# A gated scan followed by a multiplicative FFN on one core: a new hand-written order of 2,449 steps and a new split of side work between engines

## Chip, core and metric

The kernel runs on one core of one Trainium2 chip. The metric is the device time of one execution in microseconds. Three executions of the kernel before took 511.65, 510.97 and 511.06 us; their median is 511.06 us.

## What is computed

Four sequences of 5,824 tokens with 256 channels go through a gated linear recurrence (a scan in time, channel by channel), and its output through a feed-forward part with two parallel up-projections to 1,024 columns that are multiplied, then two further matrices. Cut to what matters:

```python
# scan, per channel: c = 8, a_base = sigmoid(a_param)
a_t  = exp(c * sigmoid(r_gate) * log(a_base))
xg   = sqrt(max(1 - a_t*a_t, 1e-6)) * sigmoid(i_gate) * x
h    = a_t[:, t] * h + xg[:, t];   y[:, t] = h
# feed-forward, on y as (23296, 256)
out  = ((y @ w1) * (y @ w2)) @ w3 @ w_out
```

All inputs and the output are f32; the matrix work is done in bf16.

## The kernel before

The 23,296 tokens are cut into 47 chunks: two of 256 tokens (0 and 1), 44 of 512, one of 256. A chunk's gate inputs `r`, `i` and `x` are loaded with tokens on the partitions (512 KB each). ScalarE (ACT) takes tanh of `r` and `i`; GpSimd (POOL) adds one to the tanh of `i` (`plus`) and multiplies it with `x` (`times`, L192), with VectorE (DVE) as an alternative; `th_r` and `u` are turned to channels on the partitions, by TensorE (PE, L200) for some of the first eight chunks and by a transposing DMA for all others. ACT makes the decay `a_t` by exp (L223); its square comes from POOL, DVE or ACT (`square`, L231 and L233, chosen by `DV_SQUARE` and `AC_SQUARE`); ACT takes the root (L238). Exp and tanh share a function table on ACT, the root needs another, so a switch shows as an ACT_TABLE_LOAD. DVE multiplies the root with `u` (`gated`, L248 and L251), then runs the scan, two instructions for the two halves of the channels (L270), each from the last column of the chunk before. `cast` makes `y` in bf16 (L282 on POOL or DVE, L280 on ACT).

The feed-forward part multiplies `w3 @ w_out` once, in the first 45 us (eight fold steps), into `wp_sb`. After that a chunk needs on PE eight matmul pairs for `y @ w1` (`pa`), eight for `y @ w2` (`pb`, both L299) and four strips of eight for the last product (`po`, L357). Each `pa` is copied to SBUF in bf16 (`copy`, L320 on DVE where `DV_COPY` names it, else L322 on ACT), DVE multiplies the copy with `pb` (`product`, L337), and `po` is copied out (`evac`) and stored.

Nothing schedules at run time. The string `ORDER` lists all steps; a loop at the end of the kernel runs through it and emits each step's instructions, so that the string gives the order on each engine and on SyncE's (SP) DMA queue. Each engine works strictly through its own list and waits at an instruction until its inputs are there and its buffer is free. `a5.1.0` is the `pa` matmuls of chunk 5, pair 1, half 0; `c` is its copy, `b5.1` the `pb` matmuls of that pair, `m` the product, `D` a strip of the last product, `e` its evacuation, `o` its store; `r i x` are loads, `R I p t V U` the gate steps up to the turned tiles, `d s q g h y` decay, square, root, gating, scan and cast; `Lw.. Cw..` load and cast a piece of the weights, `Ft Fc Fm Fe` fold; `W` is a pair of warming matmuls whose result nobody reads. Buffers are rings: `pa`, the turned tiles, the folds and `po` share four PSUM buffers (`po`), `pb` and the warming matmuls two (`pb`), staged weights share rings `a` and `nrm` with the decays and the roots.

Of the kernel before, what the change touches and what calls it, by code (L numbers as in the profile page):

```python
# [23 lines left out]
def kernel(  # L24
# [449 lines left out]
    def last(c):  # L474
# [26 lines left out]
        Lw3.4 x3 Lw3.3 Lw3.6 Lw3.7 r7 m0.2 h2.0 h2.1 R3 a1.2.1 a1.2.0 a0.3.0 c1.3.0 c0.3.0 Fm2 b0.3 b1.2 V3 R4 V4
        c1.2.0 d3.1 d4.0 d3.0 d4.1 m0.3 b1.3 y2 Fe2 m1.2 m1.3 a2.0.0 a2.0.1 b2.0 a2.1.0 c2.0.1 c2.0.0 c2.1.0 m2.0
        Cw3.0 s3.1 Cw3.5 Cw3.1 b2.1 a2.2.1 Ft0 a2.1.1 Fc0 Ft1 c2.1.1 Fc1 s4.0 I3 s4.1 c2.2.1 a2.2.0 Ft5 Fm0 p3 Cw3.4
        c2.2.0 Fc5 m2.1 s3.0 q3 Cw3.3 Fe0 b2.3 Fm1 q4 Fe1 Ft4 t3.0 t3.1 U3 Fc4 g3 h3.0 h3.1 Cw3.6 Cw3.7 b2.2 Fm5 Fm4
        a2.3.1 Ft7 R7 Fe5 Fe4 Fc7 r5 i4 r6 x4 i5 i6 i7 c2.3.1 a2.3.0 Ft3 R5 I4 c2.3.0 Fc3 Ft6 Fm7 y3 a3.2.1 Fc6 Fm3
# [159 lines left out]
```

## Time and profile before

| what | us |
|---|---|
| median of the three timed executions | 511.06 |
| span of the profiled execution, first to last instruction | 509.1 |
| difference, which lies around the span | 1.96 |
| PE busy (matmuls) | 501.7 |
| ACT busy | 461.5 |
| DVE busy | 431.8 |
| POOL busy | 318.0 |

How to read it: the span is one execution, recorded by the profiler; what lies around it is taken to be the same for both kernels. A busy time is the union of an engine's instructions; matmul ends are modelled. In a timeline row the first number is the start in us from the span's start, the second the length of a run of like instructions, `x` their count, and a bracket gives the idle time ahead and who ended it.

### The profile page before, as it was taken

To read this page: it belongs to the slowest core of one execution; us is meant where nothing else is said; L and a number is where in the kernel's file an instruction comes from. 1 tells how busy PE (TensorE), PEld (TensorE's weight loads), DVE (VectorE), ACT (ScalarE), POOL (GpSimd) and SP (SyncE) were. 2 spreads that over 40 slices of the span, in tenths; PEclk is the share of its full clock that TensorE was granted. 3 is DMA by queue.
4 is the path that set the end of the run, shared out by engine and by line. 5 is a ranking of instruction groups with operands and counts; after the bars stand their busy time and mean duration, and the time that the engine had idled before them with its cause. 6 is when DMAs were issued, how large, how long until landed. Compare 5 with 4: busy or idle time off the path is not lost.

```text
span 509.1 us, 8891 instructions
## 1 busy us (share of the span) xinstructions
PE 501.7 (99%) x3225; PEld 308.3 (61%) x3225; DVE 431.8 (85%) x417; ACT 461.5 (91%) x708; POOL 318.0 (62%) x269
## 2 busy tenths in 40 slices
...
GB/s 317 410 411 345 335 316 282 305 286 259 310 220 298 279 285 247 211 302 196 247 305 327 254 286 148 252 243 227 210 246 164 235 298 161 85 166 62 65 51 104
DMA packets 178048, 124.06 MB, mean 244 GB/s; under 512 B 87378, under 2 KB 174036, under 8 KB 178004
## 3 DMA queue, kind: packets, MB, share of 16 engines
...
q10 hardware_dynamic: 4, 0.00, 0.0%
...
## 4 chain that ended last, share of the span: by engine, by line
PE 92%; ACT 3%; DMA 2%; POOL 1%; DVE 1%; issue 1%; SPq 1%; ACTq 0%; DVEq 0%
PE po L357 30%; PE pb L299 29%; PE pa L299 29%; DMA wf<-in_moe_w_dram 2%; PE pw L436 1%; ACT sa L322 1%; PE ptr L200 1%; PE ptw L425 1%; POOL u_t L192 0%; DVE h_t L270 0%; SPq L151 0%; ACT ot L322 0%; SPq L407 0%; ACT L168 0%; ACT L238 0%
## 5 line engine op out<-in xcount | busy, mean ns | idle before, releaser
L337 DVE TENSOR_TENSOR g_t<-sa,pb 128x1024 bf16<-128x1024 bf16 (+1 forms) x188 | 218.7, 1180 | 58.9 <-PE pb L299 27.6
L299 PEld LDWEIGHTS <-w_sb 128*128 128x128 bf16 x1504 | 146.4, 98 | 144.1 <-issue 1.4
L322 ACT CAST sa<-pa 128x512 bf16<-128x512 f32 (+1 forms) x332 | 179.8, 591 | 27.1 <-PE pa L299 18.9
L299 PE MATMUL pa<-y_t,w_sb 128*128 128x512 bf16 (+1 forms) x752 | 190.2, 372 | 0.2 <-ACT sa L322 0.2
L299 PE MATMUL pb<-y_t,w_sb 128*128 128x512 bf16 (+1 forms) x752 | 184.9, 372 | 0.2 <-ACT w_sb L414 0.2
L357 PE MATMUL po<-wp_sb,g_t 128*128 128x256 bf16 (+1 forms) x1464 | 177.6, 272 | 0.0
L357 PEld LDWEIGHTS <-g_t 128*128 128x128 bf16 x1464 | 142.5, 98 | 39.5 <-issue 0.3
L282 POOL CAST y_t<-h_t 128x1024 bf16<-128x1024 f32 (+2 forms) x47 | 53.8, 1145 | 140.2 <-DVE h_t L270 136.1
L192 POOL TENSOR_TENSOR u_t<-i_t,x_t 128x512 bf16<-128x512 f32 (+1 forms) x90 | 123.3, 1387 | 3.8 <-DMA ut<-u_t 1.8
L270 DVE TENSOR_TENSOR_SCAN h_t<-a_t,h_t,nrm 128x512 f32<-128x512 f32 (+1 forms) x92 | 121.1, 1343 | 1.6
L233 POOL TENSOR_TENSOR nrm<-a_t 128x512 f32<-128x512 f32 x70 | 78.4, 1137 | 7.0 <-ACT a_t L223 4.0
L223 ACT ACTIVATE a_t<-rt,la 128x512 f32<-128x512 bf16 (+1 forms) x82 | 66.1, 823 | 0.0
L322 ACT COPY ot<-po 128x512 f32<-128x512 f32 x84 | 49.1, 589 | 13.2 <-PE po L357 12.9
L173 POOL TENSOR_SCALAR i_t<-i_t 128x1024 f32<-128x1024 f32 (+1 forms) x45 | 55.4, 1233 | 8.3 <-ACT i_t L168 8.3
L251 DVE SCALAR_TENSOR_TENSOR nrm<-nrm,ut 128x1024 f32<-128x1024 f32 (+1 forms) x39 | 53.2, 1365 | 5.2 <-ACT nrm L238 5.2
L168 ACT ACTIVATE i_t<-i_t 128x1024 f32<-128x1024 f32 (+1 forms) x46 | 48.5, 1063 | 0.3 <-DMA i_t<-in_i_gate_dram 0.2
L238 ACT ACTIVATE nrm<-nrm 128x1024 f32<-128x1024 f32 (+1 forms) x47 | 48.4, 1040 | 0.2
L162 ACT ACTIVATE th_r<-r_t 128x1024 bf16<-128x1024 f32 (+1 forms) x41 | 43.5, 1064 | 0.0
L320 DVE CAST sa<-pa 128x512 bf16<-128x512 f32 x36 | 23.5, 684 | 1.4 <-PE pa L299 0.8
L238 ACT ACT_TABLE_LOAD x17 | 21.8, 1283 | 0.4
L287 PE MATMUL warm<-ident 128*128 128x512 bf16 x32 | 10.7, 473 | 1.6 <-DVE ident L441 1.6
L231 ACT ACTIVATE nrm<-a_t 128x512 f32<-128x512 f32 x18 | 11.4, 645 | 0.0
...
## 6 DMA issues: line engine op xcount, KB each, us to landing
...
wf<-in_moe_w_dram SPq DMA_DIRECT2D x12, 512.0 KB, 10.5
...
rt<-th_r SPq DMA_TRANSPOSE x41, 4.7
ut<-u_t SPq DMA_TRANSPOSE x39, 4.4
```

Source lines behind the costliest of these rows:

```text
L173: (nc.vector if c in DV_PLUS else nc.gpsimd).tensor_scalar(t, t, 1.0, 1.0, op0=ALU.add, op1=ALU.mult)
L192: (nc.vector if (c, half) in DV_HALF else nc.gpsimd).tensor_mul(out=u, in0=t, in1=xt)
L223: nc.scalar.activation(out=a, in_=pr, func=AF.Exp, scale=la4[:, cb:cb + 1], bias=la4[:, cb:cb + 1])
L233: (nc.vector if (c, cb) in DV_SQUARE else nc.gpsimd).tensor_mul(out=n, in0=a, in1=a)
L238: nc.scalar.activation(out=n, in_=n, func=AF.Sqrt, scale=-1.0, bias=1.0)
L251: nc.vector.scalar_tensor_tensor(out=n, in0=n, scalar=1e-3, in1=T["pu", c][:, :, cols], op0=ALU.max, op1=ALU.mult)
L270: nc.vector.tensor_tensor_scan(h[:, cb, :], a[:, cb, :], n[:, cb, :], init, ALU.mult, ALU.add)
L282: (nc.vector if key in DV_CAST else nc.gpsimd).tensor_copy(out=y, in_=h)
L299: nc.tensor.matmul(out=dst, lhsT=w_sb[:, cb, m * P:(m + 1) * P], rhs=T["y", gates_of(c)][:, cb, span(c, mp)], start=(cb == 0), stop=(cb == ...
L322: nc.scalar.copy(out=dst, in_=src_ps)
L337: nc.vector.tensor_mul(out=T["g", z][:, 2 * mp:2 * mp + 2, span(c, mp)], in0=T["sa", c, mp][:, :, :w], in1=T["pb", c, mp][:, :, :w])
L357: nc.tensor.matmul(out=po, lhsT=T["g", c][:, k, j * P:(j + 1) * P], rhs=wp_sb[:, k, cols], start=(k == 0), stop=(k == KD - 1), skip_group_ ...
```

## The change

The 2,449 steps are the same ones, each once, before and after. Two things differ. First, `ORDER`: the first 1,399 steps stand in another order; the last 1,050, from about the third strip of chunk 23 on, stand as before. Second, the sets that choose engines. Counted over the whole program, 24 more copies of `pa` go to DVE (from 36 to 60) and as many fewer to ACT; 4 more evacuations go to DVE; 7 products of the gate go from POOL to DVE; ACT does 24 squares instead of 18, DVE 2 instead of 4, POOL the rest (4 fewer of full width); two casts of `y` of 1,024 columns go to DVE and one to ACT; ACT loads its function table 32 times instead of 34. For chunks 13 to 24 alone, `DV_COPY` names 28 copies where it named none. The number of matmuls, of transfers and of warming matmuls stays, as do ring sizes. The new file is 12 lines longer, and a line after the sets bears a number higher by three (L241 is the old L238).

The sets, and the first lines of `ORDER` on both sides:

```diff
     DV_PLUS = set()
-    DV_HALF = set()
-    DV_SQUARE = {(0, 0), (0, 1), (5, 1), (9, 0)}
-    AC_SQUARE = {(2, 0), (2, 1), (3, 0), (4, 0), (4, 1), (5, 0), (6, 0), (6, 1), (7, 0), (8, 1), (9, 1), (11, 1), (12,
-        0), (12, 1), (13, 0), (14, 1), (15, 0), (15, 1)}
-    DV_CAST = {(1, 1)}
-    AC_CAST = {(1, 0)}
-    DV_COPY = {(0, 0, 0), (0, 1, 0), (1, 0, 0), (1, 1, 0), (2, 0, 0), (2, 0, 1), (2, 1, 0), (2, 1, 1), (2, 2, 0), (2,
-        3, 0), (3, 0, 0), (3, 1, 0), (3, 3, 0), (4, 0, 1), (4, 1, 0), (4, 1, 1), (4, 3, 1), (5, 2, 1), (5, 3, 0), (6,
-        1, 0), (6, 1, 1), (6, 3, 1), (7, 2, 0), (8, 0, 0), (8, 0, 1), (8, 1, 0), (8, 2, 0), (9, 1, 1), (9, 2, 1), (9,
-        3, 0), (9, 3, 1), (10, 0, 0), (10, 3, 0), (11, 0, 1), (11, 1, 0), (12, 2, 0)}
-    DV_EVAC = {(0, 0), (0, 1), (4, 1), (5, 1), (6, 1), (9, 0), (9, 1)}
-    FOLD_ACT = {('e', 0), ('e', 4), ('e', 5), ('e', 7)}
+    DV_HALF = {(6, 1), (11, 1), (12, 1), (22, 0), (25, 0), (25, 1), (27, 0)}
+    DV_SQUARE = {(0, 1), (10, 1)}
+    AC_SQUARE = {(2, 1), (3, 0), (3, 1), (4, 0), (4, 1), (5, 1), (8, 1), (11, 1), (12, 1), (14, 1), (15, 0), (16, 1),
+        (17, 0), (17, 1), (18, 1), (19, 1), (20, 0), (20, 1), (21, 1), (22, 0), (23, 0), (25, 1), (26, 1), (28, 0)}
+    DV_CAST = {2, 23, (0, 0), (1, 0)}
+    AC_CAST = {21}
+    DV_COPY = {(0, 0, 0), (0, 1, 0), (0, 2, 0), (1, 0, 0), (1, 1, 0), (2, 0, 0), (2, 1, 1), (2, 2, 1), (3, 0, 0), (3,
+        2, 0), (3, 2, 1), (4, 0, 0), (4, 0, 1), (4, 1, 0), (4, 2, 0), (4, 3, 0), (4, 3, 1), (5, 2, 1), (6, 3, 0), (7,
+        1, 1), (7, 2, 0), (8, 2, 0), (9, 0, 0), (9, 2, 0), (10, 0, 1), (10, 1, 1), (10, 3, 1), (11, 0, 1), (11, 1, 0),
+        (11, 3, 0), (11, 3, 1), (12, 1, 0), (13, 1, 1), (14, 0, 0), (14, 1, 0), (14, 3, 0), (15, 1, 1), (15, 2, 0),
+        (16, 2, 0), (16, 2, 1), (16, 3, 0), (17, 0, 0), (17, 1, 0), (18, 1, 0), (18, 2, 0), (19, 1, 0), (19, 2, 0),
+        (19, 2, 1), (20, 0, 1), (20, 2, 1), (21, 2, 0), (22, 1, 0), (22, 1, 1), (22, 2, 0), (22, 2, 1), (23, 0, 0),
+        (23, 1, 1), (23, 2, 1), (23, 3, 0), (24, 0, 0)}
+    DV_EVAC = {(0, 0), (2, 0), (3, 0), (4, 0), (4, 1), (6, 1), (7, 0), (7, 1), (14, 0), (14, 1), (22, 1)}
+    FOLD_ACT = {('c', 4), ('c', 7), ('e', 3), ('e', 5)}
     FOLD_DMA = set()
-    W_ACT = {('w2', 0), ('w3', 3)}
-    W_DVE = {('w1', 1)}
+    W_ACT = {('w2', 1), ('wo', 1)}
+    W_DVE = set()
...
 
     ORDER = """
-        r0 i0 x0 Lw1.1 Lw1.0 r2 i2 Lw2.0 Lw3.2 x2 E W13 A3. A0. A1. A2. R0.1 R0.0 W3 W10 V0.0 V0.1 I0 t0.1 d0.0 s0.0
-        d0.1 s0.1 q0.0 t0.0 Cw1.1 q0.1 Cw1.0 R2 I2 W5 W8 W0 U0 W4 W11 W6 W12 W7 W9 W2 g0 h0.1 h0.0 y0.1 y0.0 a0.0.1
-        a0.1.1 a0.1.0 a0.0.0 V2 W15 Cw2.0 g1 h1.1 h1.0 y1.1 y1.0 d2.1 Lw2.1 Lwo.1 Lwo.0 r3 Cw3.2 d2.0 s2.1 s2.0 q2
-        b0.0 c0.0.0 c0.1.0 a1.1.0 m0.0 Ft2 a1.1.1 c1.1.0 b0.1 a1.0.0 a0.2.1 a1.0.1 b1.1 m0.1 Fc2 b1.0 a0.2.0 p2 t2.0
...
+        E W14 W4 A3. A0. W3 r0 A1. R0.0 V0.0 R0.1 V0.1 i0 I0 A2. d0.0 x0 s0.0 t0.0 W15 W12 Lw2.0 Lw1.0 W13 Cw2.0
+        W6 d0.1 s0.1 q0.0 t0.1 U0 W10 g0 Cw1.0 q0.1 g1 W9 h0.1 h0.0 y0.0 r2 R2 W5 W11 W2 V2 h1.1 i2 h1.0 y1.0
+        y0.1 a0.1.1 a0.0.1 a0.0.0 c0.0.0 y1.1 W7 Lw3.2 Cw3.2 I2 p2 d2.1 s2.1 r3 a1.1.1 a0.1.0 c0.1.0 a1.1.0 d2.0
+        c1.1.0 W8 b0.0 Lw1.1 a1.0.1 b0.1 m0.0 a1.0.0 m0.1 R3 c1.0.0 b1.1 s2.0 Ft2 b1.0 Cw1.1 q2 m1.1 a0.2.1 x2
+        m1.0 a0.2.0 c0.2.0 Fc2 V3 a1.3.1 W1 Lw2.1 Cw2.1 b0.2 a1.3.0 m0.2 d3.1 t2.0 t2.1 U2 g2 h2.0 W0 h2.1 y2
+        Lwo.0 Cwo.0 d3.0 Lwo.1 a0.3.1 Cwo.1 r4 b1.3 c1.3.0 m1.3 R4 a1.2.1 a0.3.0 c0.3.0 a1.2.0 b0.3 m0.3 Fm2 V4
+        Lw3.1 Fe2 c1.2.0 d4.1 a2.0.1 a2.0.0 c2.0.0 b2.0 Lw3.0 a2.1.0 c2.0.1 m2.0 b1.2 d4.0 Cw3.0 Cw3.1 Ft0 Fc0
...
```

First place, the first 14 us. On ACT, with what each instruction waits for: the decay of chunks 0 and 1 (`a_t`), the table load, the root (`nrm`), the table load back, tanh of chunk 2. Before:

```order
L223 ACTIVATE a_t<-ptr,la_85 128x512 [waits DVE_49,PE_49]
L223 ACTIVATE a_t<-ptr,la_85 128x512 [waits PE_49]
L238 ACT_TABLE_LOAD
L238 ACTIVATE nrm<-nrm 128x2x256 [waits DVE_49]
L238 ACTIVATE nrm<-nrm 128x2x256
L160 ACT_TABLE_LOAD
L160 ACTIVATE th_r<-r_t 128x1024 [waits DMAHW6_49]
```

Now:

```order
L226 ACTIVATE a_t<-ptr,la_85 128x512 [waits DVE_49,PE_49]
L226 ACTIVATE a_t<-ptr,la_85 128x512 [waits PE_49]
L241 ACT_TABLE_LOAD [waits DVE_49]
L241 ACTIVATE nrm<-nrm 128x2x256 [waits Pool_49]
L241 ACTIVATE nrm<-nrm 128x2x256
L163 ACT_TABLE_LOAD
L163 ACTIVATE th_r<-r_t 128x1024 [waits DMAHW6_49]
```

The table load, which waited for nothing, now waits for DVE; the root waits for POOL. On DVE at the same place, from the product of chunk 0's gates (`u_t`) over squares (`nrm<-a_t`), gating (`nrm<-nrm,ptr`) and scans (`h_t`). Before:

```order
L189 SCALAR_TENSOR_TENSOR u_t<-i_t,x_t 128x512
L233 TENSOR_TENSOR nrm<-a_t 128x512 x2
L189 SCALAR_TENSOR_TENSOR u_t<-i_t,x_t 128x512
L416 CAST w_sb<-wf 128x2x512
L248 SCALAR_TENSOR_TENSOR nrm<-nrm,ptr 128x256 x2
L270 SCALAR_TENSOR_TENSOR h_t<-a_t,nrm 128x256 x2
L248 SCALAR_TENSOR_TENSOR nrm<-nrm,ptr 128x256 x2
L270 SCALAR_TENSOR_TENSOR h_t<-a_t,h_t,nrm 128x256 x2
L282 CAST y_t<-h_t 128x256
```

Now:

```order
L192 SCALAR_TENSOR_TENSOR u_t<-i_t,x_t 128x512
L236 TENSOR_TENSOR nrm<-a_t 128x512
L192 SCALAR_TENSOR_TENSOR u_t<-i_t,x_t 128x512
L251 SCALAR_TENSOR_TENSOR nrm<-nrm,ptr 128x256 x4
L273 SCALAR_TENSOR_TENSOR h_t<-a_t,nrm 128x256 x2
L285 CAST y_t<-h_t 128x256
L273 SCALAR_TENSOR_TENSOR h_t<-a_t,h_t,nrm 128x256 x2
L285 CAST y_t<-h_t 128x256
```

One square has left DVE (POOL does it), the weight cast has left, all four gatings stand ahead of the first scan, and two casts of `y` stand on DVE behind each pair of scans.

Second place, POOL from the first casts of `y` to the product `u_t` of chunk 2, which PE turns and DVE then gates. Before:

```order
L416 CAST w_sb<-wf 128x2x512
L282 CAST y_t<-h_t 128x256 x2
L416 CAST w_t<-wf 128x1024
L173 TENSOR_SCALAR i_t<-i_t 128x1024
L192 TENSOR_TENSOR u_t<-i_t,x_t 128x512 x2
L416 CAST w_sb<-wf 128x2x512
L416 CAST wo_sb<-wf 128x1024 x2
```

Now:

```order
L236 TENSOR_TENSOR nrm<-a_t 128x512
L419 CAST w_sb<-wf 128x2x512 x2
L285 CAST y_t<-h_t 128x256 x2
L419 CAST w_t<-wf 128x1024
L176 TENSOR_SCALAR i_t<-i_t 128x1024
L236 TENSOR_TENSOR nrm<-a_t 128x512
L419 CAST w_sb<-wf 128x2x512
L195 TENSOR_TENSOR u_t<-i_t,x_t 128x512 x2
L419 CAST wo_sb<-wf 128x1024
L419 CAST w_t<-wf 128x1024 x2
```

A square of chunk 2 (`nrm<-a_t`, the second) and the cast of a piece of w1 now stand ahead of the two instructions of `u_t`; before, only the cast of w3 and the `plus` did, and the two casts of `wo` behind them are now one. In SP's queue the order of the first transfers changes with it: r0 i0 x0 w1.1 w1.0 r2 i2 w2.0 w3.2 x2 before, r0 i0 x0 w2.0 w1.0 r2 i2 w3.2 r3 w1.1 x2 now.

Third place, DVE around the scan of chunk 22. Before:

```order
L337 TENSOR_TENSOR g_t_3425<-sa_3368,pb_3446 128x1024
L337 TENSOR_TENSOR g_t_3425<-sa_3433,pb_3476 128x1024
L251 SCALAR_TENSOR_TENSOR nrm_2892<-nrm_2892,ut_3212 128x1024
L337 TENSOR_TENSOR g_t_3570<-sa_3485,pb_3529 128x1024
L337 TENSOR_TENSOR g_t_3570<-sa_3513,pb_3534 128x1024
L270 SCALAR_TENSOR_TENSOR h_t_3587<-a_t_2868,h_t_3422,nrm_2892 128x512
L337 TENSOR_TENSOR g_t_3570<-sa_3515,pb_3575 128x1024
L270 SCALAR_TENSOR_TENSOR h_t_3587<-a_t_2868,h_t_3422,nrm_2892 128x512
L337 TENSOR_TENSOR g_t_3570<-sa_3627,pb_3593 128x1024
L251 SCALAR_TENSOR_TENSOR nrm_3496<-nrm_3496,ut_3548 128x1024
```

Now:

```order
L323 CAST sa_3520<-pa_3517 128x512
L340 TENSOR_TENSOR g_t_3536<-sa_3446,pb_3526 128x1024
L323 CAST sa_3500<-pa_3523 128x512
L340 TENSOR_TENSOR g_t_3536<-sa_3500,pb_3531 128x1024
L323 CAST sa_3551<-pa_3548 128x512
L254 SCALAR_TENSOR_TENSOR nrm_3374<-nrm_3374,ut_3226 128x1024
L340 TENSOR_TENSOR g_t_3536<-sa_3520,pb_3567 128x1024
L273 SCALAR_TENSOR_TENSOR h_t_3575<-a_t_3001,h_t_3427,nrm_3374 128x512
L340 TENSOR_TENSOR g_t_3536<-sa_3551,pb_3596 128x1024
L323 CAST sa_3608<-pa_3621 128x512
L254 SCALAR_TENSOR_TENSOR nrm_3251<-nrm_3251,ut_3619 128x1024
L273 SCALAR_TENSOR_TENSOR h_t_3575<-a_t_3001,h_t_3427,nrm_3374 128x512
```

Four copies of `pa` (CAST) stand between the products on DVE, where before there was none.

## Rows read from the trace of the kernel before

**Rows 1.** The page: span, busy time by engine, chain of waits by engine.

```profile
span 509.1 us, 8891 instructions
...
PE 501.7 (99%) x3225; PEld 308.3 (61%) x3225; DVE 431.8 (85%) x417; ACT 461.5 (91%) x708; POOL 318.0 (62%) x269
...
PE 92%; ACT 3%; DMA 2%; POOL 1%; DVE 1%; issue 1%; SPq 1%; ACTq 0%; DVEq 0%
```

**Rows 2.** Stretches: from:to, length, busy PE, PEld, DVE, ACT, POOL, clock, DMA.

```profile
0.00:10.00 10.00, 7.01 (x28) 2.70 (x29) 5.28 (x19) 7.00 (x10) 0.70 (x6) 1.00 0.79 291
10.00:20.00 10.00, 9.00 (x75) 6.00 (x72) 8.96 (x18) 9.71 (x12) 6.63 (x8) 1.00 1.05 407
...
30.00:150.00 120.00, 120.00 (x824) 75.95 (x822) 117.90 (x129) 116.87 (x168) 81.46 (x67) 1.00 1.06 305
...
480.00:509.10 29.10, 25.96 (x200) 18.68 (x198) 13.83 (x16) 12.45 (x27) 0.61 (x1) 1.00 0.24 75
...
150.00:285.00 135.00, 135.00 (x827) 80.70 (x826) 116.19 (x94) 131.82 (x206) 99.09 (x80) 1.00 0.97 268
```

**Rows 3.** Waits of PE: total us, times, longest us.

```profile
PE ptr L200 <- POOL u_t L192: 0.5, 1, 0.5
```

**Rows 4.** PE in order of time: start us, length us, line, operation, count.

```profile
6.32 2.77 PE L287 MATMUL warm<-ident 128*128 128x512 bf16 x6
...
10.09 3.19 PE L287 MATMUL warm<-ident 128*128 128x512 bf16 x14
13.11 1.04 PE L299 MATMUL pa<-y_t,w_sb 128*128 128x256 bf16 x8
...
26.38 1.02 PE L299 MATMUL pa<-y_t,w_sb 128*128 128x512 bf16 x4
```

**Rows 5.** ACT in order of time, the first 13 us.

```profile
6.57 1.43 ACT L223 ACTIVATE a_t<-ptr,la 128x512 f32<-128x512 bf16 x2
8.02 1.28 ACT L238 ACT_TABLE_LOAD   x1
9.31 1.15 ACT L238 ACTIVATE nrm<-nrm 128x512 f32<-128x512 f32 x2
...
11.77 1.06 ACT L160 ACTIVATE th_r<-r_t 128x1024 bf16<-128x1024 f32 x1
```

**Rows 6.** DVE in order of time, the first 25 us.

```profile
7.69 1.29 DVE L233 TENSOR_TENSOR nrm<-a_t 128x512 f32<-128x512 f32 x2
...
9.49 0.69 DVE L416 CAST w_sb<-wf 128x1024 bf16<-128x1024 f32 x1
10.36 0.75 DVE L248 SCALAR_TENSOR_TENSOR nrm<-nrm,ptr 128x256 f32<-128x256 f32 x2 [0.18 <-PE ptr L200]
11.14 1.37 DVE L270 TENSOR_TENSOR_SCAN h_t<-a_t,nrm 128x256 f32<-128x256 f32 x2
...
14.50 0.27 DVE L282 CAST y_t<-h_t 128x256 bf16<-128x256 f32 x1
14.68 1.28 DVE L320 CAST sa<-pa 128x512 bf16<-128x512 f32 x2
...
20.94 1.28 DVE L248 SCALAR_TENSOR_TENSOR nrm<-nrm,ptr 128x512 f32<-128x512 f32 x2
...
22.73 2.49 DVE L270 TENSOR_TENSOR_SCAN h_t<-a_t,h_t,nrm 128x512 f32<-128x512 f32 x2
```

**Rows 7.** POOL in order of time, the first 20 us.

```profile
11.99 1.06 POOL L282 CAST y_t<-h_t 128x256 bf16<-128x256 f32 x2 [0.61 <-DVE h_t L270]
15.38 1.04 POOL L416 CAST w_t<-wf 128x1024 bf16<-128x1024 f32 x1 [2.33 <-DMA wf<-in_moe_w_dram]
...
17.52 2.50 POOL L192 TENSOR_TENSOR u_t<-i_t,x_t 128x512 bf16<-128x512 f32 x2
```

**Rows 8.** DVE by line, 150 to 285 us: count, busy us, mean ns, idle.

```profile
L337 DVE TENSOR_TENSOR g_t<-sa,pb 128x1024 bf16<-128x1024 bf16 x53 | 63.6, 1217 | 17.1 <-PE pb L299 7.6 <-ACT sa L322 6.6 <-PE pa L299 2.2
L270 DVE TENSOR_TENSOR_SCAN h_t<-a_t,h_t,nrm 128x512 f32<-128x512 f32 x27 | 39.8, 1488 | 0.5
```

More of the change, by code (lines that the diff above doesn't have):

```diff
@@ L501 @@
[L501 to L505, printed above, removed]
@@ new lines @@
+        b13.0 a13.0.1 c13.0.1 d19.1 s19.1 i21 D11.0 m13.0 D11.1 e11.0 a13.1.1 c13.1.1 a14.0.0 p17 t17.1 b13.1
+        I18 t17.0 c14.0.0 r22 s17.0 a13.2.1 c13.2.1 m13.1 b14.0 a14.0.1 c14.0.1 a13.2.0 a14.1.0 c13.2.0 d19.0
+        h15.0 a13.3.1 o11.0 a14.1.1 c13.3.1 h15.1 y15 m14.0 c14.1.0 b14.1 D12.1 c14.1.1 p18 V18 t18.0 U17 R20
+        s17.1 V20 I20 D12.0 b13.2 m14.1 e12.0 a13.3.0 m13.2 a14.2.1 I21 g16 c13.3.0 c14.2.1 b13.3 m13.3 R21
+        b14.2 a14.2.0 t18.1 a15.1.1 c14.2.0 d18.1 o11.1 a15.0.1 c15.0.1 a15.1.0 c15.1.0 p21 b15.0 a15.0.0
@@ new lines @@
+        o23.1 m25.2 r36 a26.0.1 c25.3.1 c26.0.0 R33 D24.2 p32 s32.1 c26.0.1 a26.1.0 U30 s29.0 s29.1 y27 d31.0
+        D24.3 e24.0 b26.0 t29.0 m25.3 e24.1 a26.2.0 a26.1.1 a26.2.1 I34 c26.1.0 b26.1 c26.2.0 V34 r35 c26.1.1
+        m26.0 g28 c26.2.1 I31 d31.1 b26.2 m26.1 m26.2 a26.3.1 a26.3.0 s31.0 h28.0 s31.1 a27.0.0 D25.0 c26.3.0
+        c26.3.1 D25.1 b26.3 m26.3 c27.0.0 a27.2.0 b27.0 a27.1.0 a27.0.1 q31 t29.1 e25.0 c27.2.0 c27.0.1 t32.0
+        a27.1.1 c27.1.0 o24.0 r40 i35 o24.1 c27.1.1 a27.3.1 q30 p31 p34 U29 h28.1 m27.0 i33 x34 b27.1 y28
```

253 lines of the change are left out of this document (127 added, 126 removed).

## Prediction

> **What bounds the kernel now.** I read the page first. PE is busy 501.7 of 509.1 us, and 92% of the chain of waits is PE [rows 1]. The reader should see that a change of order can take PE's idle time and nothing else, since its matmuls are the same ones before and after. The stretches then say where that idle time lies [rows 2]: 2.99 us in the first 10, 1.00 in the next 10, none from 30 to 150 or from 150 to 285, 3.14 in the last 29.1. The last stretch belongs to the part of the order that stays. So the idle time that the change can reach is about 4 us, all of it ahead of 30 us, and 1.6 us of that lies ahead of PE's first instruction. In the first 13 us PE also runs warming matmuls, which fill a wait and don't shorten it. The timeline shows the two paces: six warming matmuls in 2.77 us, so about 0.43 us each, and from 10.09 us fourteen in the 3.02 us up to 13.11, so 0.216 us each, which is 512 columns at 2.4 GHz [rows 4]. After that PE has no faster pace to go to.
>
> What ends the start-up is a chain over four engines, and the timelines give its links. For chunks 0 and 1: the decays on ACT at 6.57, the table load at 8.02, the root at 9.31 [rows 5], gating on DVE at 10.36, the scan of chunk 0 at 11.14 [rows 6], its casts on POOL at 11.99 [rows 7], the first real `pa` at 13.11 [rows 4]. For chunk 2: POOL's cast of w3 waits for its transfer until 15.38, the product `u_t` runs from 17.52 to 20.02 [rows 7], PE waits 0.5 us for it [rows 3], gating comes at 20.94, the scan at 22.73 [rows 6], and the first `pa` of chunk 2 at 26.38 [rows 4]. From 30 us on PE stays busy until 285 us at least [rows 2]. So I compare the two kernels by what PE has done when chunk 2 starts.
>
> **First place: the root of chunks 0 and 1.** One square moves from DVE to POOL (1.1 us there, beside the second decay, hidden). The table load now waits for the square that stays on DVE. The decays end at 8.00, the square takes 0.65 (half of 1.29 [rows 6]), so the load starts at 8.65 and not at 8.02, and ends at 9.93 with its 1.28 [rows 5]. The two halves of the root end at 10.5 and 11.1. Queued behind the load on ACT are the root, the load back, the tanh of chunk 2 and its decay; DVE's gating and PE's turn of chunk 2 wait for those. On DVE the four gatings now stand together: 0.75 for each pair [rows 6], so the scan of chunk 0 starts at 10.5 + 1.5 = 12.0 in place of 11.14 and ends at 13.4. The cast on DVE adds 0.27 [rows 6]; the other half is cast on POOL and is hidden. `y` of chunk 0 is ready at 13.6, before at 13.05. PE's order puts the turn of chunk 2 ahead of the first `pa`: root until 11.1, load back 1.28, tanh 1.06 [rows 5], so the turn (eight times 128 columns, 0.43 at the pace above) runs from 13.45 to 13.9. The first `pa` starts at about 13.95, 0.85 later than before, with the turn already behind it: a loss of 0.4 at this point, none of it yet in the end.
>
> Here a rule of the notes would give another sum. After the load at 8.02, 1.28 long, the root starts at 9.31 [rows 5], so the load costs 1.29. The Trainium skill (ScalarE: Activation LUTs, What ACT_TABLE_LOAD costs) gives about 2.66 us for each switch, because a drain is added to the load; an estimate from that page would put the root 1.4 us later still and the time near 513. The trace shows no such drain, and I go by the row.
>
> **Second place: POOL ahead of chunk 2.** The w3 piece is one transfer earlier in the queue (512 KB at 407 GB/s [rows 2] is 1.3 us), lands at about 14.1 and is no longer the wait. POOL is free of the casts of `y` at about 14.9: the first scan half of chunk 1 ends at 14.3, and a cast takes 0.53 (half of 1.06 [rows 7]). Then come the w3 cast, `plus`, and now a square and the w1 cast, about 1.0 each (the cast's 1.04 [rows 7]), so `u_t` starts at 18.9 and, with its 2.50, ends at 21.4 in place of 20.02. Its input x2 is one transfer later in the queue; before, it had landed by 17.52, so now by 18.8, hidden. The turn takes 0.43, the gating 1.28, the scan 2.49 [rows 6], directly behind one another, where before 1.0 us of other work and waits stood between the end of `u_t` and the start of the scan (2.71 less turn and gating): 21.9, 23.2, 25.65. The cast of `y` is on DVE now: the nearest row is DVE's cast of 1,024 columns, 0.69 [rows 6]. So `y` is there at 26.3, and chunk 2 starts at 26.35 against 26.38: what POOL loses, DVE gives back. But in the new order one `pb` of chunk 1 (four matmuls of 256 columns, 0.43 us) stands behind the start of chunk 2, where before it stood ahead. One more pair of warming matmuls also lies in this stretch; it fills waits. PE's work from 13.95 to there is about 11.5 us, so 0.8 us of its waits are covered by the wait for `y`. A fold step waits for the cast of `wo` that moved to ACT; that can add up to 0.4. The start therefore costs 0.4 to 0.8; I take 0.5, near the lower end, because the lower end is counted matmuls and the upper a wait that the chunk's own wait covers in part. From the other side: if the table load's wait were covered, everything up to `y` of chunk 2 comes 0.6 to 0.9 earlier, and the start gains up to 0.5. The transfers that the reordered loads start sooner or later run on one queue that is busy all this time, with the same bytes; I cost them at nothing.
>
> **Third place: DVE from 150 to 285 us.** The other moves (squares from POOL to ACT, 7 gate products and 4 evacuations to DVE, folds and weight casts swapped) lie on engines that wait for PE. The one that could reach PE is the 28 copies on DVE. With a copy at 0.64 (half of 1.28 [rows 6]) they are 17.9 us; with one cast of `y` (0.69), three evacuations (0.64 each) and a gate product (1.2 at most, as the product of a `pa` and `pb` pair [rows 8]) 21.7 us. DVE's idle time there is 135 - 116.2 = 18.8 us [rows 2]. Its scans take 1.488 there [rows 8], and 1.245 in the run of two at 22.73 [rows 6]: 27 of them hold up to 6.6 us that could go. So DVE's load becomes between 131.3 and 137.9 of 135 us: from a cost of nothing to 2.9 us. From 30 to 150 us DVE ran 117.9 of 120 us while PE was busy in all of 120.00 [rows 2]: that is the nearest row, 98% as in the lower case (131.3 of 135 is 97%), and I take nothing, with the upper end kept for the range.
>
> **Sum.** 509.1 + 0.5 = 509.6 us of span; the median of the timed runs lies 1.96 above the span of the profiled execution, so 511.5 us. A measurement of this kernel can tell about 0.2% (1.0 us) from no change; the forecast lies within that.
>
> **The rivals.**
> - *The start gains.* The load's wait is covered and the short waits go: 0.5 at the start, and of PE's 1.00 us of idle time from 10 to 20 us [rows 2] 0.7 closes: 511.1 - 1.2 = 509.9. For it: those idle times exist. Against it: the table load's wait is written in the order.
> - *DVE becomes the bound.* As DVE is handed its 28 copies and its scans don't get shorter, PE waits for products, because two `pb` buffers are all that stand between. It decides from the point where DVE's load passes 135 us; at about 2 of the 2.9 us, with the start's 0.5, 513.5. Against it: the full stretch from 30 to 150 us.
> - *Nothing moves.* The start's loss is covered by PE's wait for `y` of chunk 2 and the counted `pb` lands in another wait: 511.1.
> - *PE's pace falls.* By the rows PE ran at half pace at 6.32 and at full pace from 10.09 [rows 4], with 2.99 us of idle time in the first ten [rows 2]. In the new order the ten warming matmuls behind the turn of chunk 0 end at about 12.0 (the square ends at 9.3 with the gate product behind it, the turn at 9.8, ten at 0.216 follow), and PE then stands for 1.4 us until 13.45. If the pace fell there and stayed low for as long as at the start (about 8 us, from PE's first instruction to 10.09), 8 us would do the work of 4; 0.8 are covered: 511.5 + 3.2 = 514.7. That an idle engine falls back from 2.4 to 1.2 GHz is what the Trainium skill states (TensorE: Matmul & The Clock Gate, Part 1: The HAM clock gate); no row here shows a fall in mid-run.
>
> **Chances.** Forecast 0.47, nothing moves 0.15, start gains 0.12, DVE bound 0.21, pace falls 0.05. So faster by over 0.2% 0.12, within 0.62, slower 0.26. The range takes in the forecast with its bounds (0.5 of gain, 0.8 of loss), nothing moves, and the nearer half of DVE's case: 510.2 to 513.0.
>
> **What would show it.** In the new trace: the first table load behind the decays should start near 8.65, the first `pa` near 13.95, `u_t` of chunk 2 end near 21.4, chunk 2 start near 26.35. PE should be busy in all of 30 to 285 us. DVE busy time from 150 to 285 should be 130 to 133 us; if it is 135 and PE waits for products, the second rival holds. Wrong would be a start of chunk 2 more than 0.7 away from 26.35, or PE idle in mid-run.

## The result, and the profile of the kernel after

The changed kernel takes 513.43 us (513.27 to 514.08), the kernel before 511.06 us beside it: a ratio of 1.0045, interval 1.0033 to 1.0057. It is slower by 2.4 us, outside the range given (510.2 to 513.0), and beyond the 0.2% within which the forecast lay.

The page of the kernel after, against [rows 1]: the span, busy time by engine, and the chain of waits by engine.

```profile
span 511.5 us, 8929 instructions
...
PE 501.6 (98%) x3225; PEld 307.5 (60%) x3225; DVE 447.5 (87%) x452; ACT 452.3 (88%) x684; POOL 294.1 (58%) x256
...
PE 82%; ACT 7%; DVE 6%; issue 3%; DMA 1%; SPq 0%; DVEq 0%; ACTq 0%
```

PE's busy time is the same, the span 2.4 us longer, so the loss is time in which PE waits. Of the chain PE holds 82% in place of 92%: ACT and DVE have come into it. The stretches say where, against [rows 2] (length, then busy time of PE, PEld, DVE, ACT, POOL):

```profile
0.00:10.00 10.00, 6.23 (x30) 2.39 (x31) 4.80 (x17) 5.75 (x8) 2.88 (x8) 1.00 0.80 293
10.00:20.00 10.00, 8.35 (x71) 5.61 (x69) 8.72 (x18) 9.90 (x12) 7.50 (x9) 1.00 1.02 396
20.00:30.00 10.00, 9.37 (x81) 6.27 (x79) 9.64 (x15) 9.97 (x15) 5.54 (x5) 1.00 1.04 414
30.00:150.00 120.00, 120.00 (x824) 75.90 (x821) 117.24 (x129) 114.32 (x162) 79.64 (x70) 1.00 1.05 298
150.00:285.00 135.00, 134.44 (x822) 80.13 (x821) 130.74 (x129) 123.70 (x187) 70.34 (x61) 1.00 1.02 272
480.00:511.50 31.50, 28.43 (x219) 20.62 (x217) 14.89 (x17) 13.53 (x29) 1.49 (x3) 0.98 0.25 72
```

PE idles longer in the first 30 us (6.05 us, before 4.08); it is now idle between 150 and 285 us too (0.56 us), where before there was nothing; in the last stretch it idles 3.07 us, before 3.14. So there are two places. What each costs is read from the starts of matmuls, because idle time misleads at both: at the start the kernel after has its warming matmuls at the faster pace sooner (eight in 1.89 us from 5.66, before six in 2.77 from 6.32 [rows 4]) and idles instead, and in the middle the modelled end of the matmul ahead covers part of a gap. PE in order of time, the start, against [rows 4]:

```profile
14.03 0.62 PE L203 MATMUL ptr<-ident,th_r 128*128 128x128 bf16 x8 [1.62 <-ACT th_r L163]
14.49 0.82 PE L302 MATMUL pa<-y_t,w_sb 128*128 128x256 bf16 x6
...
27.18 1.04 PE L302 MATMUL pa<-y_t,w_sb 128*128 128x512 bf16 x4 [0.20 <-DVE y_t L285]
```

Chunk 2 starts at 27.18 and not at 26.38, and one `pb` of 0.43 us still stands behind it: 1.23 us of the 2.4. The middle of the run, PE in order of time (a run of matmuls is cut where the window asked for ends):

```profile
165.78 2.15 PE L302 MATMUL pb<-y_t,w_sb 128*128 128x512 bf16 x8
167.77 1.94 PE L302 MATMUL pa<-y_t,w_sb 128*128 128x512 bf16 x8
169.89 0.38 PE L302 MATMUL pb<-y_t,w_sb 128*128 128x512 bf16 x1 [0.18 <-DVE g_t L340]
...
181.35 1.03 PE L302 MATMUL pa<-y_t,w_sb 128*128 128x512 bf16 x4
182.54 0.71 PE L360 MATMUL po<-wp_sb,g_t 128*128 128x256 bf16 x5 [0.16 <-ACT sa L325]
...
266.73 0.59 PE L302 MATMUL pa<-y_t,w_sb 128*128 128x512 bf16 x2
267.43 0.81 PE L302 MATMUL pb<-y_t,w_sb 128*128 128x512 bf16 x3
```

A wait costs more than its bracket says. At 0.216 us for 512 columns [rows 4] the eight from 165.78 should have ended at 167.51; the next starts at 167.77, so 0.26 is lost. The same sum gives 0.39 at 169.9, 0.33 at 182.5 and 0.27 at 267.4: 1.25 us. These four are the largest; summed over every matmul from 30 to 285 us the starts lose 1.7 us after and 0.5 before, so the middle costs 1.2 net. Both places together are 2.48 by the four, and 509.1 + 2.48 + 1.96 (the forecast's distance from span to time) is 513.5.

The start on the other engines, against [rows 5 to 7]; ACT, DVE and POOL in order of time:

```profile
9.16 1.28 ACT L241 ACT_TABLE_LOAD   x1 [1.26 <-DVE nrm L236]
10.46 1.15 ACT L241 ACTIVATE nrm<-nrm 128x512 f32<-128x512 f32 x2
```

```profile
7.94 1.15 DVE L236 TENSOR_TENSOR nrm<-a_t 128x512 f32<-128x512 f32 x1 [0.30 <-ACT a_t L226]
...
26.43 0.69 DVE L285 CAST y_t<-h_t 128x1024 bf16<-128x1024 f32 x1
```

```profile
7.32 1.22 POOL L236 TENSOR_TENSOR nrm<-a_t 128x512 f32<-128x512 f32 x1 [6.02 <-ACT a_t L226]
...
13.20 0.71 POOL L285 CAST y_t<-h_t 128x256 bf16<-128x256 f32 x1 [1.64 <-DVE h_t L273]
14.78 0.77 POOL L285 CAST y_t<-h_t 128x256 bf16<-128x256 f32 x1 [0.87 <-DVE h_t L273]
...
19.56 2.51 POOL L195 TENSOR_TENSOR u_t<-i_t,x_t 128x512 bf16<-128x512 f32 x2
```

The reader should see one square of 1.15 us on DVE where the two of before took 1.29 together [rows 6], and behind it ACT idle for 1.26 us ahead of its table load. DVE by line from 150 to 285 us, against [rows 8]:

```profile
L340 DVE TENSOR_TENSOR g_t<-sa,pb 128x1024 bf16<-128x1024 bf16 x52 | 62.0, 1209 | 3.1 <-PE pb L302 1.1 <-ACT sa L325 0.8 <-ACT ot L325 0.6
L273 DVE TENSOR_TENSOR_SCAN h_t<-a_t,h_t,nrm 128x512 f32<-128x512 f32 x27 | 34.3, 1302 | 0.4
L323 DVE CAST sa<-pa 128x512 bf16<-128x512 f32 x28 | 18.6, 682 | 0.3
```

The 28 copies are there; the scans fell from 1,488 to 1,302 ns.

### The profile page after: what moved, and what is told of

It is laid out like the page before. It is cut to its first block, busy times and chain, and to the rows that moved or that the text cites. A ratio compares the mean times of both kernels' runs of the same rounds, so it can differ in the third digit from the quotient of the medians.

```text
span 511.5 us, 8929 instructions
## 1 busy us (share of the span) xinstructions
PE 501.6 (98%) x3225; PEld 307.5 (60%) x3225; DVE 447.5 (87%) x452; ACT 452.3 (88%) x684; POOL 294.1 (58%) x256
## 4 chain that ended last, share of the span: by engine, by line
PE 82%; ACT 7%; DVE 6%; issue 3%; DMA 1%; SPq 0%; DVEq 0%; ACTq 0%
PE po L360 28%; PE pb L302 26%; PE pa L302 26%; DVE h_t L273 2%; ACT sa L325 2%; DVE g_t L340 2%; PE pw L439 1%; ACT i_t L171 1%; PE ptr L203 1%; DMA i_t<-in_i_gate_dram 1%; ACT a_t L226 1%; ACT L241 1%; DVE sa L323 1%; PE ptw L428 1%; ACT th_r L165 1%
## 5 line engine op out<-in xcount | busy, mean ns | idle before, releaser
L325 ACT CAST sa<-pa 128x512 bf16<-128x512 f32 (+1 forms) x308 | 167.6, 587 | 36.1 <-PE pa L302 23.0
L285 POOL CAST y_t<-h_t 128x1024 bf16<-128x1024 f32 (+2 forms) x44 | 47.9, 1088 | 155.0 <-DVE h_t L273 132.3
L273 DVE TENSOR_TENSOR_SCAN h_t<-a_t,h_t,nrm 128x512 f32<-128x512 f32 (+1 forms) x92 | 117.0, 1305 | 1.3
L195 POOL TENSOR_TENSOR u_t<-i_t,x_t 128x512 bf16<-128x512 f32 (+1 forms) x83 | 112.7, 1373 | 1.7 <-DMA ut<-u_t 0.7
L236 POOL TENSOR_TENSOR nrm<-a_t 128x512 f32<-128x512 f32 x66 | 71.8, 1101 | 21.2 <-ACT a_t L226 17.1
L176 POOL TENSOR_SCALAR i_t<-i_t 128x1024 f32<-128x1024 f32 (+1 forms) x45 | 52.1, 1161 | 15.2 <-ACT i_t L171 15.2
L325 ACT COPY ot<-po 128x512 f32<-128x512 f32 x80 | 46.5, 584 | 13.8 <-PE po L360 13.1
L241 ACT ACTIVATE nrm<-nrm 128x1024 f32<-128x1024 f32 (+1 forms) x47 | 48.5, 1035 | 0.6 <-POOL nrm L236 0.2
L323 DVE CAST sa<-pa 128x512 bf16<-128x512 f32 x60 | 40.0, 683 | 1.9 <-PE pa L302 1.0
L234 ACT ACTIVATE nrm<-a_t 128x512 f32<-128x512 f32 x24 | 15.2, 637 | 0.2
L290 PE MATMUL warm<-ident 128*128 128x512 bf16 x32 | 9.5, 425 | 1.6 <-DVE ident L444 1.6
```

The lines of the kernel that those rows point to most:

```text
L176: (nc.vector if c in DV_PLUS else nc.gpsimd).tensor_scalar(t, t, 1.0, 1.0, op0=ALU.add, op1=ALU.mult)
L241: nc.scalar.activation(out=n, in_=n, func=AF.Sqrt, scale=-1.0, bias=1.0)
L273: nc.vector.tensor_tensor_scan(h[:, cb, :], a[:, cb, :], n[:, cb, :], init, ALU.mult, ALU.add)
L325: nc.scalar.copy(out=dst, in_=src_ps)
```

## The experiments: the start

**One square moved back, and one moved in the kernel before.** Theory: DVE's square is held up by POOL's beside it. e1 undoes the move in the kernel after, b1 makes it alone in the kernel before.

```
e1:  DV_SQUARE = {(0, 0), (0, 1), (10, 1)}      (after: {(0, 1), (10, 1)})
b1:  DV_SQUARE = {(0, 1), (5, 1), (9, 0)}       (before: {(0, 0), (0, 1), (5, 1), (9, 0)})
```

> The changed kernel with one thing altered: both squares of chunk 0 on VectorE, as in the kernel before (the changed kernel has one on GpSimd, and ScalarE's table load behind the decays waits for the other). Theory A (the start is lost at this square: beside GpSimd's square VectorE's takes 1.15 us and not 0.65, and the table load waits for it until 9.16): the load starts near 7.9, the root near 9.3, the first pa 0.8 to 1.1 us earlier than 14.49, chunk 2 starts 0.6 to 0.9 earlier than 27.18, the time is 512.5 to 512.8. Rival (the start is set by GpSimd's list ahead of chunk 2's gate product, whatever the root does): the load moves, chunk 2 still starts within 0.2 of 27.18, the time stays at 513.4.

> The kernel before with one thing altered, the mirror of the first: one square of chunk 0 goes from VectorE to GpSimd. Theory A: VectorE's square lengthens from 0.65 to about 1.15, the table load starts near 9.1 in place of 8.02, the root near 10.4, the first pa near 14.0 in place of 13.11; the time rises by 0.4 to 1.0, to 511.5 to 512.1. Rival (VectorE's 1.15 in the changed kernel is not GpSimd's doing): the square keeps 0.65, the load starts near 8.65, and the time rises by 0.3 at most.

e1 took 513.47 us (1.0041, interval 1.0028 to 1.0054), b1 511.53 us (1.0002, 0.9993 to 1.0011). DVE's squares and the table load in e1:

```profile
7.37 0.69 DVE L236 TENSOR_TENSOR nrm<-a_t 128x512 f32<-128x512 f32 x1 [1.06 <-ACT a_t L226]
...
8.03 1.28 ACT L241 ACT_TABLE_LOAD   x1
```

and the two squares in b1, POOL's and DVE's:

```profile
7.36 1.13 POOL L233 TENSOR_TENSOR nrm<-a_t 128x512 f32<-128x512 f32 x1 [6.05 <-ACT a_t L223]
...
7.98 1.05 DVE L233 TENSOR_TENSOR nrm<-a_t 128x512 f32<-128x512 f32 x1 [0.39 <-ACT a_t L223]
```

The durations answer: 0.69 us without POOL's square, 1.05 and 1.15 beside it, in either kernel. In e1 the load is back at 8.03, the start of chunk 2 at 26.60 and not 27.18. The times hardly move, against both expectations: e1 is not to be told from the kernel after, and b1 not from before. In b1 POOL's cast of the w3 piece waits for its transfer until 15.52 (15.38 in [rows 7]), so POOL's queue swallows the 0.5 and chunk 2 starts at 26.58 against 26.38. In the kernel after this transfer is early, the same cast follows the casts of `y` at once (15.50), and the delay goes through.

**The square split.** Is it POOL's instruction that DVE waits for, or a late input? g3 makes POOL's square two instructions.

```
+            cuts = [slice(0, w // 2), slice(w // 2, w)] if (c, cb) == (0, 0) else [slice(0, w)]
+            for k in cuts:
...
```

> The kernel after with POOL's square of chunk 0 as two instructions of 256 columns in place of one of 512. Theory: DVE's square took 1.15 us, not 0.65, because it stood until POOL's square of 1.22 us had ended (in three profiles it ends 0.54 to 0.55 after POOL's). Then DVE's square now starts work when POOL's first half ends, at about 7.95, and takes about 0.7, and POOL's second half ends some 0.55 after it, near 9.2; the table load waits for that and stays near 9.2. Rival: DVE's square is slow there for a reason of its own (its input comes late); then it takes 1.1 again and POOL's second half is as short as the first. The time is 513.4 in both cases; the durations are what is read.

513.11 us (1.0033, 1.0021 to 1.0045). DVE and POOL in g3:

```profile
8.14 0.69 DVE L238 TENSOR_TENSOR nrm<-a_t 128x512 f32<-128x512 f32 x1 [0.41 <-ACT a_t L226]
8.75 1.10 DVE L192 SCALAR_TENSOR_TENSOR u_t<-i_t,x_t 128x512 bf16<-128x512 f32 x1
```

```profile
7.52 1.78 POOL L238 TENSOR_TENSOR nrm<-a_t 128x256 f32<-128x256 f32 x2 [6.22 <-ACT a_t L226]
```

DVE's square is back at 0.69. POOL's two halves together now take 1.78 in place of 1.22, and DVE's `u_t` behind the square takes 1.10 in place of 0.68: it ends 0.55 after POOL's second half, as DVE's whole square ended 0.55 after POOL's (9.09 and 8.54). So the two engines take turns here, one instruction at a time. The Trainium skill (SBUF — State Buffer, SBUF: two separate sides) has this as a rule: DVE and GpSimd share a pair of ports under an exclusive lock for the whole instruction, which a DVE operation with two inputs in SBUF needs against a GpSimd operation that reads SBUF. The trace agrees: squares and `u_t` (two inputs in SBUF) wait, products `g_t` (one input in PSUM) keep 1,209 ns. The load did not stay near 9.2 as expected; it began at 8.91, behind DVE's square, while POOL's second half ran until 9.30.

**Start and rest apart.** h1 is the kernel before with the steps up to the first up-projections of chunk 2 in the order and on the engines of the kernel after; h2 is the reverse.

```
h1:  ORDER = words of after up to a2.0.1, then those of before that are left, in their order
h2:  ORDER = words of before up to a2.0.0, then those of after that are left, in their order
```

> The new start alone: the steps of the changed kernel up to the first pa of chunk 2, in their order and on their engines, then all other steps in the order and on the engines of the kernel before. By the comparison of the traces (PE's lost time up to chunk 2 is 1.25 us more): 511.06 + 1.25 = 512.3. Rival (the loss lies in mid-run, where VectorE has 28 more copies): 511.1 to 511.4.

> The old start alone: the steps of the kernel before up to the first pa of chunk 2, in their order and on their engines, then all other steps as in the changed kernel. If 1.25 us of the loss lie in the start and some 1.1 us between 140 and 270 us: 512.2. If all of it lies in the start: 511.1. If all of it lies behind the start: 513.4.

h1 took 512.81 us (1.0030, 1.0021 to 1.0040), h2 513.75 us (1.0043, 1.0031 to 1.0055). They don't add up to the change, since each has a seam: h1 a wait of 0.79 us for a product at 27.75 that neither kernel has, h2 a start of chunk 2 at 26.90, 0.5 later than before, though its start is the old one. What they do show: h1 has no wait of PE in the middle, and h2, with the old start, has those of the kernel after. PE's waits from 150 to 285 us in h2:

```profile
PE pb L303 <- DVE g_t L341: 0.5, 2, 0.3
PE po L361 <- ACT sa L326: 0.2, 1, 0.2
```

So the two losses are separate.

## The experiments: the middle

**All jobs of chunks 13 to 24 back on their old engines.** Theory: DVE's 130.7 of 135 us make the waits. e5 gives these jobs the engines of before, in after's order; b3 is the mirror; m1 and h3 are e5 with e1's squares and with h2's start.

```
e5:  DV_COPY, DV_EVAC, DV_HALF, DV_CAST, AC_CAST, AC_SQUARE: entries of chunks 13 to 24 as in before
b3:  the same entries as in after, in the kernel before
m1 = e5 + (0, 0) in DV_SQUARE        h3 = e5 + the start of h2
```

> The kernel after, in its own order, but every job of chunks 13 to 24 (copies, squares, casts, evacuations, gate products) is on the engine that it had before: 28 copies leave DVE for ACT, 10 squares leave ACT for POOL (2 come the other way). Theory: PE's waits between 150 and 285 us (about 1.4 us of lost time against none before) come from DVE's load of 130.7 of 135 us. Then DVE falls to about 115 us there, PE is busy in all of 135, and the time is 513.4 - 1.4 = 512.0. Rival: the new order of the jobs makes these waits, whatever engine does them; then PE still loses over 1 us there and the time is 513.4. Second rival: ACT, with 28 copies of 0.6 more and 10 squares less, becomes the one waited for; then it is slower than 513.4.

> The mirror: the kernel before in its own order, with the engines that the change gives to the jobs of chunks 13 to 24. Theory (DVE's load): DVE is busy some 130 of 135 us from 150 to 285, PE waits for products there and loses about 1.4 us, 512.5. Rival (the order makes the waits): 511.1 and PE busy in all of 135. Between them: the engine sets were searched for the new order, so in the old one they could cost more than 1.4, at most the 2.9 us of the prediction's upper end, 514.0.

> The kernel after with both repairs: engines of chunks 13 to 24 as before, and both squares of chunk 0 on DVE. If the two losses are separate and add, 1.4 (mid-run) and some 0.6 (the start, by the profile of the run with the squares alone, which its median did not show), 511.4. If the start's loss only moves to the start of chunk 2, 512.0. If the order makes the mid-run waits, 513.0 or more.

> The kernel before up to the first up-projection of chunk 2, then the order of the kernel after, with the engines of before for chunks 13 to 24: what is left of the change is the order from 26 us on and the engines outside these chunks. The run with the old start alone took 513.75. If the mid-run waits are DVE's load, 513.75 - 1.6 = 512.2, and what is left over 511.1 lies ahead of 60 us, where the joined order costs 1.3. If they come with the order, 513.7.

528.75 us for e5 (1.0334, 1.0314 to 1.0355), 531.91 for b3 (1.0397, 1.0381 to 1.0413), 529.12 for m1 (1.0352, 1.0329 to 1.0375), 528.49 for h3 (1.0333, 1.0317 to 1.0349). No theory had 15 to 20 us in it; of the expectations only e5's second rival, that ACT becomes the engine waited for, has the direction. The stretch from 150 to 285 us in e5, and its longest waits of PE and DVE there:

```profile
150.00:285.00 135.00, 124.82 (x737) 73.12 (x750) 104.61 (x89) 120.32 (x188) 77.94 (x67) 1.00 0.92 245
```

```profile
DVE g_t L337 <- ACT sa L322: 19.2, 13, 4.0
PE pa L299 <- ACT sa L322: 7.3, 6, 1.8
```

In these 135 us DVE is busy 26 us less than in the kernel after, ACT 3 us less, POOL stands at 78, and PE waits 7.3 us for ACT's copies alone. Over the stretch none of the three is full. Each queue runs in the written order, so a job that comes late on one engine holds up what is behind it, and through the buffers the next engine. Neither order fits the other's engines; which of the moved jobs does the harm was not tested. As a test of DVE's load, the exchange failed, because it changed the order's fit as well.

**Less work, same engines, same order.** g1 halves DVE's copies, g2 ACT's, in chunks 13 to 24: each such copy leaves out the second half of its columns, and the products of these chunks read the first half twice, at full length (1,211 and 1,209 ns in place of 1,209).

```
+        if 13 <= c <= 24 and (c, mp, q) in DV_COPY:       (g2: not in DV_COPY)
+            w = w // 2
...
+            sa = sa[:, :, :w // 2].unsqueeze(2).broadcast_to([P, 2, 2, w // 2])
```

> The kernel after, order and engines untouched; the 28 copies on DVE for chunks 13 to 24 copy only half of their columns (256 of 512), and the products of these chunks read the first half of every copied tile twice, at their full length. So DVE has some 7.5 us less to do between 150 and 285 us (28 times 0.64 less about 0.37) and no other engine has more. Theory: the 1.4 us that PE loses there come from DVE's load; then DVE is busy about 123 of 135 us, PE loses under 0.3 there, and the time is 513.4 - 1.3 = 512.1. Rival: the waits come from ACT, whose copies stand behind gate activations; then PE still loses over 1 us there and the time is 513.2 or more.

> The same with ACT's copies: those of chunks 13 to 24 that ACT does copy half of their columns, DVE's stay whole. ACT has about 15 us less to do between 150 and 285 us (some 70 times 0.57 less about 0.35), DVE as much as before, 130.7 of 135. Theory (DVE's load): the waits for products at 166 and 267 us stay, the time is 513.0 to 513.4. Rival (ACT's place in the queue): the waits go, 512.0. If both this kernel and the one with DVE's copies halved lose the waits, the chain runs over both engines by turns and either relief breaks it.

513.00 us for g1 (1.0037, 1.0025 to 1.0050), 512.63 for g2 (1.0022, 1.0013 to 1.0030). PE's waits from 150 to 285 us, g1:

```profile
PE pb L302 <- DVE g_t L346: 0.2, 1, 0.2
PE po L365 <- ACT sa L325: 0.2, 1, 0.2
```

and g2:

```profile
PE pb L302 <- DVE g_t L346: 0.3, 1, 0.3
```

With DVE at 125.22 us the waits at 167, 169.9 and 182.5 stand as they were; only the one at 267 is gone. With ACT at 112.32 us (DVE still at 131.02) those at 169.9 and 182.5 are gone, the one at 167 is left, and 0.20 is still lost at 267. So ACT's place in the chain made more of the loss than DVE's load. In the medians neither relief gave the 1.3 us that its theory asked for. But in g2's profile chunk 2 starts at 27.91 and not at 27.18, for another reason (told at the end of the next part), and the span is 511.2 us all the same, against 511.5: the middle gave back some 1.1. g1's chunk 2 starts at 27.17, its span is 511.2 too: 0.3. Five us around two of the waits, in the kernel after, fit this:

```profile
165.00:170.00 5.00, 4.71 (x22) 1.94 (x21) 4.71 (x5) 5.00 (x9) 4.05 (x4) 1.00 1.03 240
265.00:270.00 5.00, 4.89 (x28) 2.52 (x26) 5.00 (x6) 4.71 (x8) 0.00 (x0) 1.00 0.99 250
```

Around 167 and 169.9 ACT has no free moment and DVE has; around 267 it is the other way round.

**Single jobs moved.** l1 gives two copies back to ACT; x1 moves five words of the order and no engine; x2 adds e1's squares to x1; after_again repeats the kernel after beside them.

```
l1:  DV_COPY without (13, 1, 1) and (14, 0, 0)
x1:  m14.0 ahead of h15.0; g16 behind m13.3; g25 behind m23.3;
     I21 behind c14.2.1; q17 behind c16.1.0
```

> The kernel after with two copies only, those of the first pair of chunk 13 and of chunk 14 that DVE does at 157.6 and 158.2 us, given back to ACT, which stands idle for 0.5 and 1.5 us shortly after. If DVE's late products at 164 to 166 us (1.3 us of scans and copies ahead of them) make the waits at 166 to 170 us, these 0.6 us of lost time go, and the time is 512.8; the waits at 182 and 267 us stay. If ACT is the late one, 513.4 to 513.8. That it costs 10 us and more, as exchanging the engines of all 12 chunks did, would mean that no single job can be moved in this order.

> The kernel after with the same engines and five words of the order moved: the product m14.0 ahead of the scans of chunk 15 and the gating of chunks 16 and 25 behind the products m13.3 and m23.3 (DVE), the tanh I21 behind two copies and the root q17 behind two copies (ACT). Theory: PE's waits at 166, 169, 171, 182 and 267 us are the places of single jobs in two queues; they go, PE loses under 0.4 us from 150 to 285, and the time is 513.4 - 1.1 = 512.3. Rival: what is put later (a gating, a root with its table load) holds PE up in its turn one or two chunks on; then new waits of a like sum stand between 170 and 290 us and the time is 513.2 or more.

> The same, and both squares of chunk 0 on DVE. If the two losses add: 512.3 less the 0.3 that the square alone gave in the lower group of its times, 512.0. What is left over 511.3, some 0.7, is then the start behind the square. If the time falls to 511.3 or less, nothing of the start was lost. If x1 doesn't get its 1.1, 513.0.

> The kernel after, unchanged. Theory: its times fall into a lower group near 513.3 and an upper one near 514.0, by whether POOL's cast of the first w3 piece starts ahead of DVE's cast of chunk 2's output (then DVE's cast takes some 1.5 us, not 0.69, and chunk 2 starts 0.75 us later) or behind it. In its profile: a long cast on DVE goes with a POOL cast that starts first, a short one with one that starts later.

l1 took 513.52 us (1.0042, 1.0030 to 1.0055): the waits at 167, 170 and 182 us all stand, with two copies of 0.6 us less on DVE ahead of them. x1 took 516.95 us (1.0121, 1.0106 to 1.0135), x2 516.27 (1.0106, 1.0084 to 1.0127), after_again 514.05 (1.0054, 1.0042 to 1.0066). In x1 the waits at 170, 182 and 267 us are gone, as the theory said; at 166.7 and 168.7 us 0.34 and 0.26 are lost, where the theory had nothing, and the rival's new wait is there (beside a small one at 175). ACT, DVE and PE in x1, in order of time:

```profile
181.29 1.28 ACT L241 ACT_TABLE_LOAD   x1
```

```profile
183.68 1.23 DVE L254 SCALAR_TENSOR_TENSOR nrm<-nrm,ut 128x1024 f32<-128x1024 f32 x1 [2.47 <-ACT nrm L241]
...
187.38 1.20 DVE L340 TENSOR_TENSOR g_t<-sa,pb 128x1024 bf16<-128x1024 bf16 x1
```

```profile
188.63 0.59 PE L302 MATMUL pb<-y_t,w_sb 128*128 128x512 bf16 x2 [2.20 <-DVE g_t L340]
```

The root q17 stands behind two copies, its table load starts at 181.29 and not at 178.66; the gating on DVE, next in its queue, waits 2.47 us for it, a scan and the products stand behind the gating, and PE waits 2.20 us for the first of them. Two copies put ahead of one root cost more than the five words gave.

## Why the prediction was wrong

- **The bound** was read rightly: PE's work is unchanged and the time is its idle time. Both signs of being wrong that I named came: chunk 2 starts 0.83 from 26.35, and PE is idle in mid-run.
- **First place, failed step.** "the square takes 0.65" was half of a row in which both squares ran on DVE with POOL idle. Beside POOL's square it took 1.15, because it had to wait for it (e1, b1, g3). Every later time of that chain comes 0.5 late: load 9.16 (8.65 forecast), root 10.46 (9.93), first `pa` 14.49 (13.95). I had called the moved square "hidden" on POOL, and it was; its price lay on the engine that it left.
- **Second place.** The delay ran through to chunk 2. `u_t` ends at 22.07 (21.4 forecast): 0.5 from the square, the rest in POOL's casts of `y`, 0.71 and 0.77 beside DVE's scans where I took 0.53. From there to chunk 2 it took 5.11, not 4.95: it starts at 27.18 (26.35). That the cast on DVE gives back what POOL loses was right in size (0.69), but not enough. The start cost 1.23, not 0.5. e1's trace shows 0.58 of this as the square's. At the end of that trace 0.35 is left (its last strips start at 504.41, those of the kernel after at 504.76), since at 302 us 0.25 is lost again: eight `pa` from 300.65 need 1.98 us, the same eight 1.72 in the kernel after. The medians show nothing certain (513.47 against 513.43). My 11.5 us of PE's work between the first `pa` and chunk 2 were a wrong sum: the 108 matmuls of the new trace are 10.9 at full pace, so waits of 1.8 us, not 0.8, lie in that stretch.
- **Third place, failed step.** DVE's load came out at 130.74 us, inside the 130 to 133 that I named. But I took 0 for it, since a stretch at 98% had cost nothing, and the middle cost 1.25. The term was read from a sum of busy time; the loss comes from the place of single jobs. g1 (0.3 given back), l1 and x1 show that DVE's load is not what decides; g2 (some 1.1) shows ACT's queue in the larger part. Which job on ACT it is stays open. The rival "DVE becomes the bound" (513.5) gave nearly the time that came by luck: it wanted a load past 135 us, and DVE idled 4.26 of the 135, full only in places such as that at 267.
- **The scans** got shorter, 1,488 to 1,302 ns, as the lower case of the load assumed. POOL is busy for 70 us there in place of 99, so fewer of them can meet it; that this is the cause was not tested.
- **The table load.** Its root starts 1.30 us after it again (9.16 and 10.46). The Trainium skill's drain of 1.4 us (ScalarE: Activation LUTs, What ACT_TABLE_LOAD costs) does not show.
- **The pace** didn't fall in the kernel after: PE waited 1.62 us ahead of 14.03, and the six matmuls of 256 columns from 14.49 take 0.11 us each, full pace. But the rival was no empty one: in the profiles of l1 and b3 the pace did fall at longer waits of PE, of 2.03 and 4.84 us (rows in the last part).

Still open: the start of the kernel after differs from one execution to the next. Its ten times lie at 513.24 to 513.43 or at 513.98 to 514.75 us, and two things that lengthen the start are on record. In three profiles of kernels with this start (e5, g2, x1) DVE's cast of chunk 2's `y` was long, 1.38 to 1.55 us, and POOL's cast of a w3 piece had begun first. In g2:

```profile
26.30 1.55 DVE L285 CAST y_t<-h_t 128x1024 bf16<-128x1024 f32 x1
...
26.27 2.48 POOL L424 CAST w_t<-wf 128x1024 bf16<-128x1024 f32 x2 [3.35 <-DMA wf<-in_moe_w_dram]
```

In the profiles of the kernel after DVE was first by less than 0.1 us, and its cast took 0.69. Which comes first hangs on a transfer, and chunk 2 starts some 0.7 us later if POOL does. The other is in l1, whose start is that of the kernel after:

```profile
8.88 1.10 POOL L419 CAST w_sb<-wf 128x1024 bf16<-128x1024 f32 x1 [0.34 <-DMA wf<-in_moe_w_dram]
...
9.01 1.52 DVE L192 SCALAR_TENSOR_TENSOR u_t<-i_t,x_t 128x512 bf16<-128x512 f32 x1
...
10.59 0.81 PE L203 MATMUL ptr<-ident,u_t 128*128 128x128 bf16 x6 [2.03 <-DVE u_t L192]
11.19 3.73 PE L290 MATMUL warm<-ident 128*128 128x512 bf16 x10
```

There POOL's cast of a weight began ahead of DVE's `u_t` (in the kernel after 0.03 behind it, 9.04), `u_t` took 1.52 in place of 0.68, PE waited for it, and the ten warming matmuls ran at a lower pace, 3.73 in place of 2.32. Chunk 2 starts at 27.65, and the run took 513.83. Both profiled runs of the kernel after lie in the lower group; but x1's profiled run had the long cast and was the fastest of its four, so that these two make the groups is not shown.
